# Routing of a fused attention, expert and feed-forward kernel: logits summed in PSUM, traced earlier

## The chip, the cores and the metric

One core of a Trainium2 chip runs the whole program. The metric is the device time of one execution in microseconds (us), lower is better; a profiled execution also has a trace of every instruction on TensorE (PE and its weight loads, PEld), VectorE (DVE), ScalarE (ACT), GpSimd (POOL) and the DMA-issuing queues (SP and ACT).

## The reference, cut to what matters

Three layers follow one another on 2304 tokens (4 batches of 576) of width 512. The routing of the second layer is what the change touches.

```python
# 1. attention with random features: q, k, v of shape (4, 8, 576, 64)
x = attn_out.transpose(0, 2, 1, 3).reshape(2304, 512)
# 2. experts: one of 8 per token, by the largest logit
logits = x @ w_gate                                # (2304, 8)
expert_idx = np.argmax(logits, axis=1)
probs = np.exp(logits - logits.max(-1, keepdims=True))
probs /= probs.sum(-1, keepdims=True) + 1e-09
gate_w = probs[np.arange(N), expert_idx]
for e in range(8):
    mask = expert_idx == e
    out[mask] = gate_w[mask, None] * (np.maximum(x[mask] @ w1[e], 0) @ w2[e])
# 3. feed-forward: h = y @ w_in; g = h * sigmoid(1.702 h); g @ w_out
```

## The kernel before, in words

The kernel works batch by batch and assumes that most tokens of a batch go to one expert: `route(b)` finds the expert that most of the 576 tokens chose, SyncE (the SP queue) reads its number into a register, and the weights of that expert alone are loaded and used for the whole batch. Tokens that chose another expert are counted in `total` and handled by a loop at the end, which runs only if there are any.

Attention is cut into 8 quads (a batch has two): `kgen(i)` makes the keys' side of a quad and `qgen(i)` the queries' side, in the order of the string `Q_ORDER`, where P is a projection with its row maximum (`ph_P`), X a transposition, N the product with its division, R the transposition into the expert layer's input (`xh`, `xl`). Each P step passes small results through the tile `small`, one whole PSUM bank with tag "t": its reduction writes there and two tensor operations read or write there (lines 359 and 368). Tag "n" is one other PSUM bank; `num` of the N steps, `kv_ps` of the keys, half of `lT_ps`, and in the routing `lg_ps` and `ct_ps` take it in turn, so each waits until the one before has been read. Tag "u" is a third one, shared by `tq`, `tx` and the other half of `lT_ps`.

Routing of batch b (`route_steps`) runs once both quads of the batch are done. It multiplies the inputs with the two halves of the gate weights (`wgs`, a rounded part and the rest, so 16 rows for 8 experts) into `lT`, turns `lT` with five transposes into `lg_ps` (tokens on partitions), copies that to SBUF, clears the 64 partitions of the last tile that hold no token, adds the two halves to `lg`, takes the row maximum `rm` and the one-hot `oh`, counts with a matmul by ones into `ct_ps`, and takes the index of the largest count (`es`). The gates (a softmax, `ex` and `gate`) and a per-token index (`lix`, five pairs of `max` and `max_index`) come along the way. Only after all this does the trace call `values_load` of `es` and `pump()`, which asks for the weights.

Two generators are interleaved by hand: attention `A` (with the routings) and the expert layer `Mg`. Inside attention `merge` takes the part that has the smallest ratio of steps taken to its weight: 17 for `qgen`, `ROUTE_N` for the routing, 5 for `kgen`. So `ROUTE_N = 10` spreads the routing's seven steps over the first six tenths of a quad; a larger number puts them closer to its start. Until the first routing is traced, only attention is traced; what has been traced by then is the `lead`, and from there on attention and experts alternate by cost. Routings of batches 0, 1 and 2 are merged into quads 2, 4 and 6; that of batch 3 follows all quads.

The order on each engine is not the traced one. The framework's scheduler plays the program through with its own durations, takes on each engine what is ready, and among that what was traced first; the order that it finds is then fixed, and each engine keeps to it, waiting in place where something is late. The SP queue carries the loads, the stores, the turning of the halves (`dma_start_transpose`, line 309), the register read and the loads of the expert weights, all in one such order. Loads of the first batch's weights are marked as high priority (`HP_STAGE`).

Of the kernel before, what the change touches and what calls it, by code (L numbers as in the profile page):

```python
# [8 lines left out]
F32 = mybir.dt.float32  # L9
# [13 lines left out]
def kernel(  # L23
# [13 lines left out]
    nc = tc.nc  # L37
    B, H, S, D = q.shape
    M = omega.shape[0]
    E, DM, F1 = w1.shape  # L40
    F2 = w_in.shape[1]
    NT = B * S
    P = 128
    T = 4
    TAIL = S - T * P
# [16 lines left out]
    XQ = nc.sync  # L62
    DVE_LO = 1
    KPRE = 6
    ROUTE_N = 10
    HP_ROUTE = 0
    HP_SPLIT = (0, 3)
    HP_STAGE = (0,)
# [438 lines left out]


    gate_t, reg_t = {}, {}

    def route(b):
        g = route_steps(b)
# [7 lines left out]
    def route_steps(b):  # L520
        yield 0
        xh, xl = xh_t[b], xl_t[b]
        lT = att.tile([2 * E, S], F32, tag="dg", name="lT", bufs=1)
        for hf, tg in ((0, "n"), (1, "u")):
            c = slice(hf * HS, (hf + 1) * HS)
            lT_ps = pp.tile([2 * E, HS], F32, tag=tg, name="lT_ps", bufs=1)
            for kk in range(KD):
                wk = wgs[:, kk].rearrange("p a e -> p (a e)")
                nc.tensor.matmul(out=lT_ps, lhsT=wk, rhs=xh[:, kk, c], start=(kk == 0), stop=False)
                nc.tensor.matmul(out=lT_ps, lhsT=wk, rhs=xl[:, kk, c], start=False, stop=(kk == KD - 1))  # L530
            nc.scalar.activation(out=lT[:, c], in_=lT_ps, func=ACTF.Copy)
        yield 2.0
        yield 0
        lg_ps = pp.tile([P, T + 1, 2, E], F32, tag="n", name="lg_ps", bufs=1)
        for t in range(T + 1):
            n = P if t < T else TAIL
            nc.tensor.transpose(
                lg_ps[:n, t].rearrange("p a e -> p (a e)"), lT[:, t * P:t * P + n], ident[:2 * E, :2 * E]
            )
        lg2 = att.tile([P, T + 1, 2, E], F32, tag="lg2", name="lg2", bufs=1)  # L540
        nc.vector.memset(lg2[:, T], 0.0)
        nc.vector.tensor_copy(lg2[:, 0:T], lg_ps[:, 0:T])
        nc.vector.tensor_copy(lg2[:TAIL, T], lg_ps[:TAIL, T])
        lg = att.tile([P, T + 1, E], F32, tag="lg", name="lg", bufs=1)
        nc.vector.tensor_tensor(out=lg, in0=lg2[:, :, 0], in1=lg2[:, :, 1], op=ALU.add)


        rm = att.tile([P, T + 1, 1], F32, tag="rm", name="rm", bufs=2)
        nc.vector.tensor_reduce(out=rm, in_=lg, axis=AX.X, op=ALU.max)
        oh = att.tile([P, T + 1, E], F32, tag="oh", name="oh", bufs=2)  # L550
        nc.vector.tensor_tensor(out=oh, in0=lg, in1=rm.to_broadcast([P, T + 1, E]), op=ALU.is_equal)
        nc.vector.memset(oh[TAIL:, T, :], 0.0)
        ex = att.tile([P, T + 1, E], F32, tag="ex", name="ex", bufs=2)
        nc.vector.tensor_tensor(
            out=ex, in0=lg, in1=rm.to_broadcast([P, T + 1, E]), op=ALU.subtract
        )
        nc.scalar.activation(out=ex, in_=ex, func=ACTF.Exp)
        yield 0.5
        yield 0
        ct_ps = pp.tile([P, T + 1, E], F32, tag="n", name="ct_ps", bufs=1)  # L560
        nc.tensor.matmul(
            out=ct_ps.rearrange("p t e -> p (t e)"), lhsT=ones, rhs=oh.rearrange("p t e -> p (t e)")
        )
        ct = att.tile([P, E], F32, tag="ct", name="ct", bufs=2)
        nc.vector.tensor_reduce(out=ct, in_=ct_ps.rearrange("p t e -> p e t"), axis=AX.X, op=ALU.add)
        cm = att.tile([P, 8], F32, tag="cm", name="cm", bufs=2)
        ci = att.tile([P, 8], U32, tag="ci", name="ci", bufs=2)
        nc.vector.max(cm, ct)
        nc.vector.max_index(ci, cm, ct)
        es = att.tile([P, 1], I32, tag="es", name="es", bufs=B)  # L570
        nc.vector.tensor_copy(es, ci[:, 0:1])
        gate = att.tile([P, T + 1, 1], F32, tag="gate", name="gate", bufs=2)
        nc.vector.tensor_reduce(out=gate, in_=ex, axis=AX.X, op=ALU.add)
        nc.vector.tensor_scalar(out=gate, in0=gate, scalar1=1e-9, scalar2=None, op0=ALU.add)
        nc.vector.reciprocal(out=gate, in_=gate)
        if b == B - 1:
            dg = att.tile([P, T * P + TAIL], F32, tag="dg", name="dg", bufs=1)
            for t in range(T + 1):
                n = P if t < T else TAIL
                nc.scalar.activation(  # L580
                    out=dg[:n, t * P:t * P + n], in_=ident[:n, :n], func=ACTF.Copy, scale=gate[:n, t, :]
                )
        cif = att.tile([P, 1], F32, tag="cif", name="cif", bufs=2)
        nc.vector.tensor_copy(cif, ci[:, 0:1])
        mx = att.tile([P, T + 1, 8], F32, tag="lmx", name="lmx", bufs=1)
        ix = att.tile([P, T + 1, 8], U32, tag="lix", name="lix", bufs=1)
        for t in range(T + 1):
            nc.vector.max(mx[:, t], lg[:, t])
            nc.vector.max_index(ix[:, t], mx[:, t], lg[:, t])
        ixf = att.tile([P, T + 1, 1], F32, tag="ixf", name="ixf", bufs=1)  # L590
        nc.vector.tensor_copy(ixf, ix[:, :, 0:1])
        eq = att.tile([P, T + 1, 1], F32, tag="eq", name="eq", bufs=1)
        nc.vector.tensor_scalar(out=eq, in0=ixf, scalar1=cif[:, 0:1], scalar2=None, op0=ALU.is_equal)
        nc.vector.memset(eq[TAIL:, T, :], 0.0)
        rr = att.tile([P, T + 1, 2], F32, tag="rr", name="rr", bufs=2)
        nc.vector.scalar_tensor_tensor(
            out=rr[:, :, 0:1], in0=eq, scalar=-float(2 * E), in1=ixf, op0=ALU.mult, op1=ALU.add
        )
        hit = att.tile([P, 1], F32, tag="hit", name="hit", bufs=1)
        nc.vector.tensor_reduce(out=hit, in_=eq.rearrange("p t o -> p (t o)"), axis=AX.X, op=ALU.add)  # L600
        nc.vector.tensor_tensor(out=total, in0=total, in1=hit, op=ALU.subtract)
        nc.vector.tensor_copy(rr[:, :, 1:2], gate)
        yield 0.5
        reg_t[b] = nc.values_load(
            es[0:1, 0:1], engines=[mybir.EngineType.SP], min_val=0, max_val=E - 1,
            skip_runtime_bounds_check_because="an index of the largest of E counts",
        )
        pump()
        nc.sync.dma_start(
            out=r_dram[b * S:b * S + T * P].rearrange("(p t) c -> p t c", t=T), in_=rr[:, 0:T]  # L610
        )
        nc.sync.dma_start(out=r_dram[b * S + T * P:(b + 1) * S], in_=rr[:TAIL, T])
        gb = moe.tile([P, S], F32, tag="gb", name="gb", bufs=2)
        if b < B - 1:
            row = att.tile([P, P, T + 1], F32, tag="dg", name="row", bufs=1)

            def leave():
                behind(nc.scalar.dma_start(out=gate_dram[b].rearrange("(p t) -> p t", p=P), in_=gate[:, :, 0]), 1)

# [24 lines left out]
        yield 1.1
# [355 lines left out]
    if True:  # L1000
# [544 lines left out]
```

## Time and profile before

| | us |
|---|---|
| three runs | 767.65, 767.72, 769.79 |
| median | 767.72 |
| the profiled execution | 767.65 |
| its span, first to last instruction | 765.6 |
| PE busy in the span | 739.7 |
| DVE busy | 531.3 |
| ACT busy | 338.6 |
| POOL busy | 131.9 |

The profiled execution has 2.05 us outside its span. Mean granted TensorE clock is 0.990. A busy PE is not a PE at its peak: matmuls are pipelined, and their ends are modelled. A duration of a single matmul is longer than the distance to the next one, so distances are taken from the chain, where each piece begins at the end of the piece before it.

### The profile page before, as it was taken

How to read it: one execution, taken by the hardware profiler on the slowest of the kernel's cores; microseconds unless marked ns; L12 is line 12 of the kernel's file. 1: busy time of each engine (PE TensorE's matmuls, PEld its weight loads, DVE VectorE, ACT ScalarE, POOL GpSimd, SP SyncE). 2: the span in 40 equal slices, each digit the busy share in tenths (PEclk: the TensorE clock that was granted, in tenths of full speed). 3: DMA queues.
4: the chain of work that ended last, by engine and by line, in shares of the span. 5: the costliest groups of instructions: out<-in, count | busy, mean ns of one | idle time of the engine just before them, and what ended most of it. 6: DMA issues, size and time to landing. Idle time of an engine off the chain costs nothing.

```text
span 765.6 us, 14359 instructions
## 1 busy us (share of the span) xinstructions
PE 739.7 (97%) x5559; PEld 716.1 (94%) x5559; DVE 531.3 (69%) x1188; ACT 338.6 (44%) x638; POOL 131.9 (17%) x78
## 2 busy tenths in 40 slices
PE   7998799999999999989999999999999999999997
PEld 6877699999999999979999999999999999999996
DVE  5867867586776685556879559981368777777774
ACT  5554464335522332233427464554576433444331
POOL 3563377609500441000000000000000000000000
PEclk9999799999999999999999999999999999999999
DMA  5447594456725554198145558972978544443311
GB/s 157 117 131 187 123 302 97 120 140 193 189 60 162 150 179 134 51 234 287 59 161 197 177 171 295 316 263 100 332 273 298 172 138 138 137 129 117 115 29 32
DMA packets 136715, 127.57 MB, mean 167 GB/s; under 512 B 58176, under 2 KB 120896, under 8 KB 135744
## 3 DMA queue, kind: packets, MB, share of 16 engines
q1 hardware_dynamic: 123936, 98.85, 43.5%
q10 hardware_dynamic: 12704, 27.73, 10.3%
q8 instruction: 45, 0.74, 0.4%
q14 instruction: 30, 0.25, 0.1%
HBM read 79.68 MB, written 40.40 MB: 157 GB/s over the span
## 4 chain that ended last, share of the span: by engine, by line
PE 83%; DVE 8%; DMA 4%; issue 1%; ACT 1%; SPq 1%; POOL 0%; ACTq 0%; POOLq 0%; DVEq 0%
PE m_ps L136 19%; PE qa L1249 13%; PE qa L1146 13%; PE qm L1249 7%; PE w_ps L136 4%; PE pb L1249 3%; PE qm L1146 3%; PE qu L1146 3%; PE num L444 3%; PE kv_ps L402 3%; DMA st<-in_moe_w_dram 2%; PE qn L1146 2%; PE qt L1146 2%; PE tq L430 1%; PE pr L344 1%
## 5 line engine op out<-in xcount | busy, mean ns | idle before, releaser
L1146 PE MATMUL qa<-y,wi 128*128 128x384 f32 x576 | 109.2, 337 | 0.4 <-DVE g L901 0.4
L1146 PEld LDWEIGHTS qa<-y,wi 128*128 128x128 f32 x576 | 101.4, 188 | 0.8 <-DVE g L901 0.8
L136 PE MATMUL m_ps<-xh,wh 128*128 128x288 f32 x256 | 79.0, 309 | 4.1 <-DVE h1l L735 2.3
L136 PE MATMUL m_ps<-xh,wl 128*128 128x288 f32 x256 | 76.8, 300 | 0.1
L136 PE MATMUL m_ps<-xl,wh 128*128 128x288 f32 x256 | 76.4, 298 | 0.0
L700 POOL TENSOR_TENSOR wl<-st,wh 128x1024 fp32r<-128x1024 f32 x23 | 55.1, 2401 | 83.0 <-ACT wh L698 82.9
L359 DVE TENSOR_REDUCE small<-pr 128x4 f32<-128x512 f32 (+1 forms) x80 | 51.1, 639 | 11.8 <-PE pr L351 7.8
L698 ACT ACTIVATE wh<-st 128x1024 fp32r<-128x1024 f32 (+1 forms) x33 | 34.0, 1035 | 48.5 <-DMA st<-in_moe_w_dram 31.6
L136 PEld LDWEIGHTS m_ps<-xh,wh 128*128 128x128 f32 x256 | 48.6, 190 | 5.8 <-DVE h1l L735 3.6
L136 PE MATMUL m_ps<-h1h,wh 128*128 128x288 f32 x160 | 48.8, 305 | 0.9 <-DVE h1l L735 0.9
L136 PEld LDWEIGHTS m_ps<-xh,wl 128*128 128x128 f32 x256 | 48.6, 190 | 0.5 <-DVE wl L700 0.4
L735 DVE SCALAR_TENSOR_TENSOR h1l<-m_ps,h1h 128x288 fp32r<-128x288 f32 x64 | 28.9, 453 | 28.9 <-ACT h1h L732 28.8
L136 PEld LDWEIGHTS m_ps<-xl,wh 128*128 128x128 f32 x256 | 48.6, 190 | 0.0
L136 PE MATMUL m_ps<-h1l,wh 128*128 128x288 f32 x160 | 47.7, 298 | 0.0
L136 PE MATMUL m_ps<-h1h,wl 128*128 128x288 f32 x160 | 47.4, 298 | 0.0
L732 ACT ACTIVATE h1h<-m_ps 128x288 fp32r<-128x288 f32 x64 | 25.9, 407 | 48.5 <-PE m_ps L136 46.7
L1249 PE MATMUL qa<-p,p 128*128 128x256 f32 x360 | 46.2, 282 | 1.1 <-DVE p L855 0.8
L1249 PE MATMUL qa<-p,gs 128*128 128x256 f32 x360 | 45.9, 282 | 0.0
L1249 PEld LDWEIGHTS qa<-p,p 128*128 128x128 f32 x360 | 44.2, 189 | 1.6 <-DVE p L855 1.0
L1249 PEld LDWEIGHTS qa<-p,gs 128*128 128x128 f32 x360 | 44.2, 189 | 0.0
L444 PEld LDWEIGHTS num<-kv,qpT 128*128 128x128 f32 (+1 forms) x320 | 36.7, 184 | 5.4 <-ACT qpT L432 3.1
L444 PE MATMUL num<-kv,qpT 128*128 128x65 f32 (+1 forms) x320 | 39.3, 266 | 2.5 <-ACT qpT L432 1.4
(213 smaller groups left out, 1819.5 us busy)
## 6 DMA issues: line engine op xcount, KB each, us to landing
g_dram<-g ACTq DMA_DIRECT2D x48, 384.0 KB, 4.1
st<-in_moe_w_dram SPq DMA_DIRECT2D x31, 512.0 KB, 5.2
pg<-g_dram SPq DMA_DIRECT2D x10, 1024.0 KB, 5.7
raw<-in_moe_w_in_dram SPq DMA_DIRECT2D x16, 512.0 KB, 4.0
gt<-g_dram SPq DMA_DIRECT2D x8, 1024.0 KB, 5.4
p<-wo_dram SPq DMA_DIRECT2D x6, 1024.0 KB, 7.3
yt<-y_dram SPq DMA_DIRECT2D x12, 384.0 KB, 6.0
vm<-in_v_dram SPq DMA_DIRECT2D x32, 128.0 KB, 3.2
```

What stands on the lines that cost most here:

```text
L136: ins = nc.tensor.matmul(out=ps, lhsT=a, rhs=b, start=start and n == 0, stop=stop and n == 2)
L344: nc.tensor.matmul(out=ps[:, :, h2], lhsT=xT[:, (2 * pr + h2) * 2 + t0 // 2], rhs=wbd)
L359: nc.vector.tensor_reduce(out=pm, in_=ps[:, :w], axis=AX.X, op=ALU.max, negate=on_act)
L402: nc.tensor.matmul(out=kv_ps[:, h, :], lhsT=kp[j // 2][:, j % 2, h2, :], rhs=vm[:, h, t, :], start=(t == 0), stop=False,)
L430: nc.tensor.transpose(tq[:, c, h2], qp[i][:, c, h2, :], ident)
L444: nc.tensor.matmul(out=ps[:n, c, h2, :], lhsT=lhsT, rhs=kv[:, h, :])
L698: nc.scalar.activation(out=hi[:, :, s], in_=st[:, :, s], func=ACTF.Copy)
L700: eng.tensor_tensor(out=lo[:, :, s], in0=st[:, :, s], in1=f32(hi)[:, :, s], op=ALU.subtract)
L732: nc.scalar.activation(out=hh[:, f], in_=ps, func=ACTF.Relu)
L735: nc.vector.scalar_tensor_tensor(out=hl[:, f], in0=ps, scalar=0.0, in1=f32(hh[:, f]), op0=ALU.max, op1=ALU.subtract)
L1146: ins = nc.tensor.matmul(out=ps, lhsT=w[:, a, ks], rhs=y[:, b, kk], start=start and kk + m == 0, stop=kk == 1 and m == 2, skip_group_check ...
L1249: ins = nc.tensor.matmul(out=ps, lhsT=x[:, f], rhs=w[i][:, f], start=start and f + m == 0, stop=f == NP - 1 and m == 2, skip_group_check=True,
```

## The change

Logits: five transposes of `lT` become five matmuls of `lT` with `fold`, a 16x8 matrix of two identities, which turns and adds the two halves at once; the result stays in PSUM, in columns 256 to 295 of `small`, and the maximum, the one-hot and the gates' subtraction read it there. `lT` is widened to 640 columns and the last 64 are cleared, so nothing has to be cleared behind it. Counts: a matmul over the first four tiles and one over the 64 real tokens of the last, into columns 384 to 423 of `small`. The register read and `pump()` move up, directly behind `es`; the gates come after them. The per-token index comes from the one-hot by a multiplication with 8, 7, ... 1 and a maximum (`left`) instead of five pairs of `max` and `max_index`. `ROUTE_N` goes from 10 to 40. Two small operations at the start of the program make `fold` and `left`.

```diff
-    ROUTE_N = 10
+    ROUTE_N = 40
...
+    lgx = att.tile([P, 2, E], F32, name="lgx")
+    fold, left = lgx[:2 * E, 0], lgx[:, 1]
+
+    def setup_route():
+        nc.vector.tensor_tensor(out=fold, in0=ident[:2 * E, 0:E], in1=ident[:2 * E, E:2 * E], op=ALU.add)
+        nc.vector.tensor_scalar(out=left, in0=iota8, scalar1=-1.0, scalar2=float(E), op0=ALU.mult, op1=ALU.add)
...
-        lT = att.tile([2 * E, S], F32, tag="dg", name="lT", bufs=1)
+        lT = att.tile([2 * E, (T + 1) * P], F32, tag="dg", name="lT", bufs=1)
+        nc.vector.memset(lT[:, S:], 0.0)
...
-        lg_ps = pp.tile([P, T + 1, 2, E], F32, tag="n", name="lg_ps", bufs=1)
+        lg_ps, ct_ps = (
+            small[:, x:x + (T + 1) * E].rearrange("p (t e) -> p t e", e=E) for x in (2 * P, 3 * P)
+        )
         for t in range(T + 1):
-            n = P if t < T else TAIL
-            nc.tensor.transpose(
-                lg_ps[:n, t].rearrange("p a e -> p (a e)"), lT[:, t * P:t * P + n], ident[:2 * E, :2 * E]
-            )
-        lg2 = att.tile([P, T + 1, 2, E], F32, tag="lg2", name="lg2", bufs=1)
-        nc.vector.memset(lg2[:, T], 0.0)
-        nc.vector.tensor_copy(lg2[:, 0:T], lg_ps[:, 0:T])
-        nc.vector.tensor_copy(lg2[:TAIL, T], lg_ps[:TAIL, T])
-        lg = att.tile([P, T + 1, E], F32, tag="lg", name="lg", bufs=1)
-        nc.vector.tensor_tensor(out=lg, in0=lg2[:, :, 0], in1=lg2[:, :, 1], op=ALU.add)
+            nc.tensor.matmul(out=lg_ps[:, t], lhsT=lT[:, t * P:(t + 1) * P], rhs=fold)
...
-        nc.vector.memset(oh[TAIL:, T, :], 0.0)
...
-        ct_ps = pp.tile([P, T + 1, E], F32, tag="n", name="ct_ps", bufs=1)
         nc.tensor.matmul(
-            out=ct_ps.rearrange("p t e -> p (t e)"), lhsT=ones, rhs=oh.rearrange("p t e -> p (t e)")
+            out=ct_ps[:, 0:T].rearrange("p t e -> p (t e)"), lhsT=ones, rhs=oh[:, 0:T].rearrange("p t e -> p (t e)")
         )
+        nc.tensor.matmul(out=ct_ps[:, T], lhsT=ones[:TAIL, :], rhs=oh[:TAIL, T])
...
         nc.vector.tensor_copy(es, ci[:, 0:1])
+        reg_t[b] = nc.values_load(es[0:1, 0:1], engines=[mybir.EngineType.SP], ...)
+        pump()
+        ex = att.tile([P, T + 1, E], F32, tag="ex", name="ex", bufs=2)
+        nc.vector.tensor_tensor(out=ex, in0=lg_ps, in1=rm.to_broadcast([P, T + 1, E]), op=ALU.subtract)
+        nc.scalar.activation(out=ex, in_=ex, func=ACTF.Exp)
...
-        for t in range(T + 1):
-            nc.vector.max(mx[:, t], lg[:, t])
-            nc.vector.max_index(ix[:, t], mx[:, t], lg[:, t])
         ixf = att.tile([P, T + 1, 1], F32, tag="ixf", name="ixf", bufs=1)
-        nc.vector.tensor_copy(ixf, ix[:, :, 0:1])
+        nc.vector.tensor_tensor(out=oh, in0=oh, in1=left.unsqueeze(1).to_broadcast([P, T + 1, E]), op=ALU.mult)
+        nc.vector.tensor_reduce(out=ixf, in_=oh, axis=AX.X, op=ALU.max)
+        nc.vector.tensor_scalar(out=ixf, in0=ixf, scalar1=-1.0, scalar2=float(E), op0=ALU.mult, op1=ALU.add)
...
-        reg_t[b] = nc.values_load(es[0:1, 0:1], engines=[mybir.EngineType.SP], ...)
-        pump()
...
         setup_wg()
+        setup_route()
```

## Rows read from the trace of the kernel before

**Rows 1.** The page, busy time and share of the span by engine.

```profile
PE 739.7 (97%) x5559; PEld 716.1 (94%) x5559; DVE 531.3 (69%) x1188; ACT 338.6 (44%) x638; POOL 131.9 (17%) x78
```

**Rows 2.** Busy time of each engine by stretch, then granted clock, DMA share, GB/s.

```profile
73.50:79.00 5.50, 4.38 (x48) 3.61 (x47) 4.94 (x18) 3.98 (x10) 4.90 (x3) 1.00 0.05 10
79.00:86.00 7.00, 4.90 (x41) 4.04 (x39) 6.92 (x43) 2.57 (x8) 3.50 (x3) 0.76 0.38 87
86.00:95.00 9.00, 5.94 (x43) 5.05 (x43) 5.92 (x27) 3.24 (x11) 0.00 (x0) 0.79 0.71 170
95.00:98.00 3.00, 2.98 (x14) 2.83 (x15) 2.06 (x6) 2.74 (x8) 0.33 (x1) 0.50 1.04 349
...
110.00:270.00 160.00, 160.00 (x1422) 154.02 (x1421) 110.14 (x358) 64.38 (x123) 69.61 (x33) 1.00 0.53 144
...
330.00:350.00 20.00, 17.56 (x124) 16.65 (x125) 13.63 (x23) 6.35 (x10) 0.00 (x0) 1.00 0.89 235
```

**Rows 3.** The chain that ended last, around the first routing: start, us, what.

```profile
73.41 0.70 ACT lT L531 x2
...
77.91 0.06 PE pr L350
...
78.25 0.38 PE lg_ps L537 x5
...
88.35 0.06 DVE es L571
...
89.22 4.37 DMA st<-in_moe_w_dram
...
95.02 2.77 PE m_ps L136 x10
...
98.42 0.45 PE num L444 x4
```

**Rows 4.** PE in order of time; idle before and its releaser in brackets.

```profile
75.55 1.11 PE L444 MATMUL num<-kv,qpT 128*128 128x65 f32 x8 [0.75 <-ACT qpT L432]
...
80.01 1.08 PE L444 MATMUL num<-kv,qpT 128*128 128x65 f32 x8 [0.83 <-DVE small L368]
...
84.98 0.39 PE L561 MATMUL ct_ps<-oh,ones 128*128 128x40 f32 x2 [0.76 <-DVE xn L455]
...
94.30 0.40 PE L136 MATMUL m_ps<-xh,wh 128*128 128x288 f32 x1 [1.73 <-ACT wh L698]
```

**Rows 5.** DVE in order of time.

```profile
74.42 0.70 DVE L359 TENSOR_REDUCE small<-pr 128x4 f32<-128x512 f32 x1
...
75.36 0.16 DVE L368 TENSOR_TENSOR mx<-small,sq 128x4 f32<-128x4 f32 x1
...
77.11 0.42 DVE L455 TENSOR_TENSOR xn<-num,rd 128x256 f32<-128x256 f32 x1
...
79.90 1.35 DVE L545 TENSOR_TENSOR lg<-lg 128x40 f32<-128x40 f32 x1
...
84.42 0.42 DVE L455 TENSOR_TENSOR xn<-num,rd 128x256 f32<-128x256 f32 x1
```

**Rows 6.** The SP queue in order of time.

```profile
82.01 5.73 SPq L309 DMA_TRANSPOSE xT<-hl  x2
```

**Rows 7.** What the SP queue waited for, 72 to 90 us: total, times, longest.

```profile
SPq L309 <- PE pr L351: 11.3, 2, 9.4
```

**Rows 8.** The tile lg, all four routings: ns min/median/max, first and last start.

```profile
L588 DVE MAX8 lmx<-lg x20: 145/153/160, 81.4 to 317.0; 128x8 f32<-128x8 f32 x20
L589 DVE MATCH_VALUE_LOAD lix<-lmx,lg x20: 71/73/88, 82.7 to 318.2; 128x8 f32 x20
L589 DVE FIND_INDEX8 lix<-lmx,lg x20: 154/160/171, 82.8 to 318.3; 128x8 uint32<-128x8 f32 x20
```

**Rows 9.** Groups by line and shape: count, busy us, mean ns, idle before, releaser.

```profile
L700 DVE TENSOR_TENSOR wl<-st,wh 128x1024 fp32r<-128x1024 f32 x8 | 9.8, 1224 | 7.1 <-ACT wh L698 7.1
```

More of the change, by code (lines that the diff above doesn't have):

```diff
@@ L533, in route_steps @@
         yield 0
-        lg_ps = pp.tile([P, T + 1, 2, E], F32, tag="n", name="lg_ps", bufs=1)
+        lg_ps, ct_ps = (
+            small[:, x:x + (T + 1) * E].rearrange("p (t e) -> p t e", e=E) for x in (2 * P, 3 * P)
+        )
         for t in range(T + 1):
-            n = P if t < T else TAIL
-            nc.tensor.transpose(
-                lg_ps[:n, t].rearrange("p a e -> p (a e)"), lT[:, t * P:t * P + n], ident[:2 * E, :2 * E]
-            )
-        lg2 = att.tile([P, T + 1, 2, E], F32, tag="lg2", name="lg2", bufs=1)
-        nc.vector.memset(lg2[:, T], 0.0)
-        nc.vector.tensor_copy(lg2[:, 0:T], lg_ps[:, 0:T])
-        nc.vector.tensor_copy(lg2[:TAIL, T], lg_ps[:TAIL, T])
-        lg = att.tile([P, T + 1, E], F32, tag="lg", name="lg", bufs=1)
-        nc.vector.tensor_tensor(out=lg, in0=lg2[:, :, 0], in1=lg2[:, :, 1], op=ALU.add)
+            nc.tensor.matmul(out=lg_ps[:, t], lhsT=lT[:, t * P:(t + 1) * P], rhs=fold)
         rm = att.tile([P, T + 1, 1], F32, tag="rm", name="rm", bufs=2)
-        nc.vector.tensor_reduce(out=rm, in_=lg, axis=AX.X, op=ALU.max)
+        nc.vector.tensor_reduce(out=rm, in_=lg_ps, axis=AX.X, op=ALU.max)
         oh = att.tile([P, T + 1, E], F32, tag="oh", name="oh", bufs=2)
-        nc.vector.tensor_tensor(out=oh, in0=lg, in1=rm.to_broadcast([P, T + 1, E]), op=ALU.is_equal)
-        nc.vector.memset(oh[TAIL:, T, :], 0.0)
[L553 to L557, printed above, removed]
+        nc.vector.tensor_tensor(out=oh, in0=lg_ps, in1=rm.to_broadcast([P, T + 1, E]), op=ALU.is_equal)
         yield 0.5
         yield 0
-        ct_ps = pp.tile([P, T + 1, E], F32, tag="n", name="ct_ps", bufs=1)
         nc.tensor.matmul(
-            out=ct_ps.rearrange("p t e -> p (t e)"), lhsT=ones, rhs=oh.rearrange("p t e -> p (t e)")
+            out=ct_ps[:, 0:T].rearrange("p t e -> p (t e)"), lhsT=ones, rhs=oh[:, 0:T].rearrange("p t e -> p (t e)")
         )
+        nc.tensor.matmul(out=ct_ps[:, T], lhsT=ones[:TAIL, :], rhs=oh[:TAIL, T])
         ct = att.tile([P, E], F32, tag="ct", name="ct", bufs=2)
@@ L571, in route_steps @@
         nc.vector.tensor_copy(es, ci[:, 0:1])
+        reg_t[b] = nc.values_load(
+            es[0:1, 0:1], engines=[mybir.EngineType.SP], min_val=0, max_val=E - 1,
+            skip_runtime_bounds_check_because="an index of the largest of E counts",
+        )
+        pump()
+        ex = att.tile([P, T + 1, E], F32, tag="ex", name="ex", bufs=2)
+        nc.vector.tensor_tensor(
+            out=ex, in0=lg_ps, in1=rm.to_broadcast([P, T + 1, E]), op=ALU.subtract
+        )
+        nc.scalar.activation(out=ex, in_=ex, func=ACTF.Exp)
         gate = att.tile([P, T + 1, 1], F32, tag="gate", name="gate", bufs=2)
@@ L584, in route_steps @@
         nc.vector.tensor_copy(cif, ci[:, 0:1])
-        mx = att.tile([P, T + 1, 8], F32, tag="lmx", name="lmx", bufs=1)
-        ix = att.tile([P, T + 1, 8], U32, tag="lix", name="lix", bufs=1)
-        for t in range(T + 1):
-            nc.vector.max(mx[:, t], lg[:, t])
-            nc.vector.max_index(ix[:, t], mx[:, t], lg[:, t])
         ixf = att.tile([P, T + 1, 1], F32, tag="ixf", name="ixf", bufs=1)
-        nc.vector.tensor_copy(ixf, ix[:, :, 0:1])
+        nc.vector.tensor_tensor(out=oh, in0=oh, in1=left.unsqueeze(1).to_broadcast([P, T + 1, E]), op=ALU.mult)
+        nc.vector.tensor_reduce(out=ixf, in_=oh, axis=AX.X, op=ALU.max)
+        nc.vector.tensor_scalar(out=ixf, in0=ixf, scalar1=-1.0, scalar2=float(E), op0=ALU.mult, op1=ALU.add)
         eq = att.tile([P, T + 1, 1], F32, tag="eq", name="eq", bufs=1)
@@ L603, in route_steps @@
         yield 0.5
[L604 to L607, printed above, removed]
-        pump()
         nc.sync.dma_start(
```

## The prediction

> **What bounds the kernel now.** I began with the page's busy table: TensorE works in 97% of the span, no other engine in more than 69% [rows 1]. So a change can save only where TensorE stands or runs at its lower clock, and costs wherever it adds TensorE work to a stretch that is already full. The table by stretches then shows where that is [rows 2]. From 110 to 270 us TensorE is busy 160.00 of 160.00 us at clock 1.00; nothing is to be won there. Around the first routing it is not: from 73.5 to 79 it is busy 4.38 of 5.50, from 79 to 86 4.90 of 7.00 at clock 0.76, from 86 to 95 5.94 of 9.00 at clock 0.79, and the first expert matmuls run at 0.50, which is 1.2 of 2.4 GHz. VectorE is busy 6.92 of 7.00 from 79 to 86, so attention alone can't fill TensorE there: it is bound by VectorE. The second loose place is 330 to 350, with 20.00 - 17.56 = 2.44 us idle.
>
> The chain through the first place says what ends last [rows 3]. `lT` is evicted by 74.11. The five transposes follow only at 78.25, the index `es` is made at 88.35, the weights are asked for at 89.22 and land 4.37 us later, and the expert stream sets in at 95.02. TensorE's own timeline shows it standing for these weights last (1.73 us before 94.30) [rows 4]. From the end of `lT` to `es` are 14.2 us for operations that take some 2 us themselves.
>
> Why they take so long is read off TensorE's and VectorE's timelines together. `num` of the first N step takes the "n" bank at 75.55 [rows 4] and is read out by VectorE from 77.11 to 77.53 [rows 5]; only then can `lg_ps` have the bank, 4 us after `lT` is there. The next `num` waits 0.83 us in turn for the copies out of `lg_ps`, and the count matmul waits 0.76 us for the division that ends at 84.84 [rows 4, 5]. In between the add of the two halves takes 1.35 us [rows 5], and the operations of P steps that were traced earlier take their turns on VectorE.
>
> **The change part by part.**
>
> *Off the "n" bank, and traced earlier.* With a weight of 40 the logits are traced behind the second P step of the quad and the counts behind the first X step, ahead of the N steps; in `small` no `num` has to be read out first. I take it that logits must still wait for the P steps traced before them, since these use the same bank: the third of them ends at 75.36 + 0.16 = 75.52 [rows 5]. From there: ten TensorE instructions (an f32 matmul appears as two, as the counts do [rows 4]) at 0.11 us each, from `num`'s 0.45 for 4 [rows 3], are 1.1; maximum, one-hot, count reduction and `es` at some 0.17 us each, the price of such small operations (`max` 0.153, index 0.160, load 0.073 [rows 8]), with one index search come to 1.1; four count instructions 0.4. Waiting behind one VectorE operation of up to 0.70 us [rows 5] at each of four hops is 0 to 2.8, and I take 1.2. `es` is then made at about 79.3 instead of 88.35, 9 us earlier; the bounds are 7 and 10. The register read and eight weight loads come with it, and the expert stream sets in at about 86.0.
>
> *What the shift is worth.* In 86 to 95 TensorE's busy time at the granted clock is 5.94 x 0.79 = 4.7 us, so 4.3 are free; by counting, its 43 instructions at 0.06 to 0.11 us apart [rows 3] are 2.6 to 4.7, so 4.3 to 6.4 are free. Expert matmuls, which need nothing but weights, fill that: I take 4.9. If the shift is 7 us, 3.3. The ten slow matmuls at 95.02 (2.77 us) I expect again, at the new place, since the stretch ahead of them stays sparse; if the clock stays up, 1.4 more is gained.
>
> *VectorE's work.* Per routing go five `max` and index pairs, 5 x (0.153 + 0.073 + 0.160) = 1.93 us [rows 8], two copies, two memsets, one cast and the add, some 0.8 more by the prices of small operations, and for the first routing the add's long 1.35 [rows 5]. A memset, a multiplication, a reduction and a scalar operation come in, 0.6. So 2.1 us a routing, 3.3 in the first. Where TensorE is full this is worth nothing, since VectorE is off the path. In 73.5 to 86, where VectorE is the bound, attention comes forward by up to 3.3 us, which at 4.90 x 0.76 us of TensorE work in 7.00 [rows 2] is 1.7 at most; as the experts soon fill that stretch anyway, I take 1.0.
>
> *TensorE's added work.* Five transposes at 0.38 [rows 3] become ten instructions: 0.76 if each takes as long as a transpose, 1.1 at `num`'s price; the counts go from two instructions to four, 0.15 to 0.22. That is 0.5 to 0.9 a routing. In the first it falls into free time; the other three lie where TensorE is full [rows 2]: 1.6 to 2.8, and I take 2.0.
>
> *Reading logits in PSUM, gates behind the index, two setup operations.* Gates are first needed at the end of the experts' first stage, half a batch away, and the setup is two small operations at the program's start; nothing, or 0.3 us if the start stands for them. The SP queue now has the register read and the weight loads ahead of what was traced later, its two turned-halves transfers above all (82.01 to 87.74 [rows 6]); these serve the next quads and may start some 3 us later, which the expert matmuls cover. Without that cover they would delay the next P step by as much, up to 3 us.
>
> *Last routing.* It stays behind all quads in the trace, so only its own shortening counts. Of the 2.44 us idle at 330 to 350 I take 1.0 back; bounds 0 and 2.4.
>
> *Waits on `small`.* Logits and counts on TensorE stand behind VectorE's use of that bank, and P steps behind theirs. The waits on "n" that go were 0.83 and 0.76; I take 0.5 us more in the full stretches, bounds 0 and 6 x 1.1 (a whole P step, 74.42 to 75.52 [rows 5]).
>
> Sum: -4.9 - 1.0 + 2.0 - 1.0 + 0.5 = -4.4 us. The profiled execution took 767.65, which gives 763.2; it lies 0.07 below the median shown, so the same number serves for both.
>
> **The rivals.** *The SP queue keeps the old place.* The two transfers at line 309 stand at its head, waiting 9.4 us for P matmuls to free a buffer [rows 7], and the second ends at 87.74 [rows 6]. If the scheduler leaves the register read behind them, the early index is worth under 1 us of shift, 0.5 us of time, and the sum is -0.5 - 1.0 + 2.0 - 1.0 + 0.5: 767.7, no change. For it: they were traced first. Against it: they wait until 82.0, and the index should be there at 79.3 with loads of high priority. Between the two transfers the shift would be about 4 us, and 765.
>
> *The shared bank becomes the wait: slower.* Each P step now locks TensorE's logits and counts and is locked by them. In the six places of the last three routings TensorE keeps its order and would stand for a P step (1.1 us) and, where one is ahead of it, a long VectorE operation (1.22 [rows 9]), with all expert matmuls queued behind. From 0.8 us a place (4.9 in all, where 0.5 was taken) the gain is gone; at 1.5 us it is 763.2 + 8.5 = 771.7. For it: at 80 and 85 us TensorE did stand 0.83 and 0.76 for exactly such a hand-over. Against: the scheduler puts an instruction where it expects it to be ready, and in 110 to 270 TensorE never stands, although "n" is shared in the same way.
> The Trainium skill speaks for this rival: PSUM — Partial Sum Buffer, "PSUM bank collisions raise a hardware error", asks that two engines be kept apart by bank and quadrant, not by address, so different columns of `small` don't make logits and P steps independent. Were the rule not applied here, logits could start at 74.15 rather than 75.52, and the sum would be some 0.7 us lower. No row here shows two engines in that bank at once, which agrees with the rule and doesn't prove it.
>
> *The new order costs elsewhere.* All that is traced after the lead moves (the lead is about ten trace steps shorter), so prefetches and hand-overs fall differently; either sign, some 2 us.
>
> **How the numbers follow.** Forecast 0.57 (its own range 760.0 to 765.5), SP queue 0.18 (765 to 768.5), bank 0.15 (768.5 to 772), new order 0.10, half of it at each side of no change. 0.3%, 2.3 us, is about what a measurement of this kernel can tell from no change: the three runs differ by 2.1. Faster by more than that, below 765.4: most of the forecast, a little of the SP rival and of the last: 0.59. Slower, above 770.0: most of the bank and a part of the last: 0.16. Between: 0.25. The range leaves out the strongest form of the bank rival and the very best: bounds at their best (-6.4 for the shift, -1.7, +1.6, -1.0) give 760.1, and with the clock up 758.7; I take 759.5 to 769.0.
>
> **What would show it.** Right: no wait of `num` or `ct_ps` for the "n" bank; `es` near 79 and the first weights asked for near 80, ahead of line 309 on SP; the first expert matmul near 85 instead of 94.30; TensorE's idle time from 73.5 to 98 some 4 us shorter; logits as ten instructions in about 1 us. Wrong: weights still asked for behind 87 (the queue); TensorE idle in 110 to 270 ahead of `small` (the bank); or that stretch kept and the saved time gone again before 350.

## The result, and the profile after

The rebuilt routing is slower: 778.87 us, the median of 4 runs (777.09 to 781.43), against 767.68 of before, ratio 1.0141, 95% interval [1.0112, 1.0169]. Forecast was 763.2. The profiled execution took 777.57 with a span of 775.6, 10.0 more than before.

The page of the kernel after, and the stretches of [rows 2] (us, busy PE, PEld, DVE, ACT, POOL, then granted clock, DMA share, GB/s):

```profile
PE 746.7 (96%) x5587; PEld 723.4 (93%) x5587; DVE 520.3 (67%) x1122; ACT 337.2 (43%) x638; POOL 131.7 (17%) x78
```

```profile
73.50:79.00 5.50, 4.72 (x27) 3.09 (x25) 3.55 (x10) 2.53 (x5) 3.60 (x4) 0.69 0.16 36
79.00:86.00 7.00, 6.39 (x43) 6.06 (x43) 3.64 (x19) 1.78 (x6) 5.86 (x3) 0.61 0.01 2
86.00:95.00 9.00, 6.98 (x45) 6.07 (x45) 7.48 (x34) 3.91 (x9) 0.49 (x1) 0.55 0.74 234
95.00:98.00 3.00, 3.00 (x29) 3.00 (x28) 2.04 (x4) 3.00 (x6) 3.00 (x2) 1.00 1.06 389
110.00:270.00 160.00, 154.38 (x1364) 147.41 (x1364) 98.79 (x322) 59.94 (x116) 62.65 (x30) 0.99 0.56 138
330.00:350.00 20.00, 20.00 (x151) 19.75 (x150) 15.81 (x47) 9.69 (x21) 0.00 (x0) 1.00 0.72 210
```

The clock had fallen before the first logits, in a stretch of 2 us from 74 on:

```profile
74.00:76.00 2.00, 2.00 (x11) 1.02 (x9) 1.83 (x5) 0.80 (x2) 1.92 (x2) 0.50 0.26 58
```

Read against [rows 2]: from 79 to 86 VectorE, which was full there (6.92 of 7.00), is busy 3.64; the clock is 0.55 to 0.69 for 21 us where it was 0.76 to 1.00 (the next 3 us run at 1.00 where they ran at 0.50); and 110 to 270, full before, has 5.6 us idle. TensorE has 28 instructions more, seven for each routing.

TensorE, then VectorE, around the first routing (start, us, engine, line, operation; in brackets the idle time ahead and what ended it):

```profile
75.37 0.33 PE L350 MATMUL pr<-wh,xT 128*128 128x128 f16 x1
...
77.92 1.11 PE L444 MATMUL num<-kv,qpT 128*128 128x65 f32 x8 [0.75 <-ACT qpT L432]
78.95 1.28 PE L545 MATMUL small<-lgx,lT 16*128 16x8 f32 x10
...
82.39 0.58 PE L552 MATMUL small<-oh,ones 128*128 128x32 f32 x2
82.90 0.59 PE L555 MATMUL small<-oh,ones 64*128 64x8 f32 x2
...
86.79 0.27 PE L350 MATMUL pr<-wh,xT 128*128 128x128 f16 x1 [1.40 <-DVE qp L380]
...
88.62 1.10 PE L444 MATMUL num<-kv,qpT 128*64 128x65 f32 x8 [0.82 <-DVE xn L455]
...
90.13 0.61 PE L136 MATMUL m_ps<-xh,wh 128*128 128x288 f32 x1 [0.41 <-ACT wh L692]
```

```profile
80.27 0.20 DVE L547 TENSOR_REDUCE rm<-small 128x5 f32<-128x40 f32 x1 [0.37 <-PE small L545]
80.50 0.20 DVE L549 TENSOR_TENSOR oh<-small,rm 128x40 f32<-128x40 f32 x1
83.53 0.20 DVE L557 TENSOR_REDUCE ct<-small 128x8 f32<-128x40 f32 x1 [2.83 <-PE small L555]
83.65 0.19 DVE L570 TENSOR_TENSOR ex<-small,rm 128x40 f32<-128x40 f32 x1
83.75 1.32 DVE L588 TENSOR_TENSOR oh<-oh,lgx 128x40 f32<-128x40 f32 x1
85.00 0.16 DVE L560 MAX8 cm<-ct 128x8 f32<-128x8 f32 x1
85.08 0.41 DVE L359 TENSOR_REDUCE small<-pr 128x2 f32<-128x256 f32 x1
...
85.87 0.14 DVE L563 CAST es<-ci 128x1 int32<-128x1 uint32 x1
```

`es` comes at 85.87, some 2.4 us earlier than before (88.26 on VectorE's timeline), not 9. VectorE stands 2.83 us for the counts. The next P reduction, which writes the same bank, comes only at 85.08, although its matmuls began at 75.37; TensorE then stands 1.40 us for the `qp` of that P step. VectorE's waits on routing results in the whole run (total us, times, longest):

```profile
DVE rm L547 <- PE small L545: 7.0, 3, 5.1
DVE ct L557 <- PE small L555: 4.3, 3, 2.8
```

One more difference lies ahead of the routing altogether. The turnings of the halves on SP's queue, first before, then after, in two quads of the attention that come before any routing:

```profile
57.34 1.89 SPq L309 DMA_TRANSPOSE xT<-hl  x1
...
61.00 2.40 SPq L309 DMA_TRANSPOSE xT<-hl  x1
```

```profile
56.88 2.73 SPq L309 DMA_TRANSPOSE xT<-hl  x1
...
60.77 3.31 SPq L309 DMA_TRANSPOSE xT<-hl  x1
```

Nothing in the order of the instructions explains that; e7 to e12 below look for the cause.

All is lost before the feed-forward layer: its first matmul starts at 400.4 before and 410.7 after, and the rest takes 365.2 and 364.9. What the time up to that matmul consists of, from stretches of 2 us each: idle TensorE, time lost at the lower clock (length x (1 - granted clock)), and the remainder, which is TensorE's work at full clock. There is one profile of each kernel, and runs of one kernel differ by some 3 to 10 us, so a difference of 1 or 2 us in a column says little.

| kernel | idle | lost at lower clock | work |
|---|---|---|---|
| before | 18.7 | 6.8 | 374.9 |
| after | 22.1 | 12.0 | 376.7 |
| e1, weight 40 alone | 17.8 | 6.8 | 370.8 |
| e5, e1 with the shared bank | 22.2 | 6.8 | 373.4 |
| e9, e14, one-hot index, `hl` on its boundary | 20.2, 19.2 | 6.8, 5.1 | 373.3, 373.3 |
| e4, after with banks n and u | 19.0 | 10.3 | 377.4 |
| e11, after, `hl` on its boundary | 22.0 | 8.5 | 376.8 |
| e12, the same with banks n and u | 17.7 | 6.8 | 378.7 |
| e13, TensorE's part alone | 18.0 | 10.2 | 378.1 |

### The profile page after: what moved, and what is told of

Same layout as the page of the kernel before. It is cut to its first block, busy times and chain, and to the rows that moved or that the text cites. A ratio compares the mean times of both kernels' runs of the same rounds, so it can differ in the third digit from the quotient of the medians.

```text
span 775.6 us, 14360 instructions
## 1 busy us (share of the span) xinstructions
PE 746.7 (96%) x5587; PEld 723.4 (93%) x5587; DVE 520.3 (67%) x1122; ACT 337.2 (43%) x638; POOL 131.7 (17%) x78
## 4 chain that ended last, share of the span: by engine, by line
PE 80%; DMA 9%; DVE 4%; ACT 2%; SPq 2%; issue 2%; POOL 0%; ACTq 0%; DVEq 0%
PE m_ps L136 16%; PE qa L1244 13%; PE qa L1141 13%; PE qm L1244 7%; DMA st<-in_moe_w_dram 5%; PE w_ps L136 4%; PE pb L1244 3%; PE qm L1141 3%; PE qu L1141 3%; PE num L444 3%; DMA m<-in_q_dram 2%; PE tq L430 2%; PE kv_ps L402 2%; PE qn L1141 2%; PE pr L344 2%
```

## The experiments

Ratios are to the kernel before, run beside each kernel on the same chip, with 95% intervals; e1 to e4 ran on one chip, e5 to e8 on a second, e9 to e15 on a third. There were three theories at first: Q (the order of SP's queue costs the time), B (the bank that the routing shares with the P steps), T (the work added on TensorE and VectorE).

Four pairs below turn out to be the same program twice. Where an edit only moves `values_load` and `pump()` in the source (e3 against after, e6 against e1, e8 against e4, e14 against e9), the scheduler puts the register read and the loads back where they were. In the built programs the two kernels of a pair have the same instructions in the same order on every engine, and their traces show SyncE's instructions and TensorE's matmuls in the same order (after and e3: 623 and 5587). Their ratios differ by up to 0.3% (1.0141 and 1.0113), so smaller differences between two ratios are not taken for effects here.

**e1: the weight alone.** Before, with one line changed.

```diff
-    ROUTE_N = 10
+    ROUTE_N = 40
```

> The kernel before with ROUTE_N = 40 alone; routing as it was. Theory Q (the register read and the eight weight loads go onto the SP queue ahead of the two line-309 transfers, so the next quads' data come late and attention starves from 110 us): those transfers are issued near 93 and 100 us instead of 82 and 86, TensorE idles 4 to 6 us between 110 and 270, and the time is 775 to 780. Theory B (logits and counts in the bank of the P steps are the cost): no change of bank here, so 765 to 769. Theory T (added TensorE and changed VectorE work is the cost): 765 to 769.

763.47 (7 runs), ratio 0.9975 [0.9944, 1.0005]. The register read comes at 81.7, the first expert matmul at 85.98 instead of 94.30, and the turnings at line 309 start at 90.24 and 97.98 instead of both from 82.01 on [rows 6]. So the old routing, traced earlier, brings the expert matmuls 8 us forward by itself, and turnings 8 us late cost no time on the whole. The gain is 2 us, not the 4.9 that the prediction gave to such a shift, and by this run alone it is not clear of noise (e6, the same program, is). In the trace the free time moved forward and was not filled. Ahead of the counts TensorE now stands 5.01 us for the one-hot, and from 73 to 100 it loses 10.8 us idle or at the lower clock, against 11.4 before.

```profile
77.60 0.62 PE L561 MATMUL ct_ps<-oh,ones 128*128 128x40 f32 x2 [5.01 <-DVE oh L552]
```

**e2: all but the weight.** After, with one line changed back.

```diff
-    ROUTE_N = 40
+    ROUTE_N = 10
```

> The changed kernel with ROUTE_N = 10; all of the rebuilt routing stays. Theory Q: the scheduler has both line-309 transfers ahead of the register read again, so 764 to 769, faster than before by what the shorter routing is worth. Theory B: logits and counts still lie in the bank of the P steps, so 774 to 780. Theory T: the added TensorE work is still there, 769 to 772.

777.27, ratio 1.0139 [1.0112, 1.0166], as slow as after, although the turnings start at 82.01 and 87.82 as before, ahead of the register read. Theory Q falls with e1 and e2 together.

**e3: the register read late.** After, with `values_load` and `pump()` where they were.

```diff
@@ behind es
-        reg_t[b] = nc.values_load(es[0:1, 0:1], ...)
-        pump()
@@ behind the last yield, ahead of the stores to r_dram
+        reg_t[b] = nc.values_load(es[0:1, 0:1], ...)
+        pump()
```

> The changed kernel with the register read and the weight loads traced behind the gates, where they were before; ROUTE_N stays 40. Theory Q: the read stands ahead of the line-309 transfers on SP as in the changed kernel, so 775 to 780, no gain. A theory that the early read within the routing is the cost expects 765 to 769. Theory B: 775 to 780 as well.

774.53, ratio 1.0113 [1.0080, 1.0147]. This is the program of after once more, so it can't tell what an early read costs, only how far two measurements of one program lie apart. It also means that one part of the change, the read moved up in the source, had no effect.

**e4: own banks** (as the labels call them: logits go to n, which `num` uses too, and counts to u, which `tq` uses too).

```diff
-        lg_ps, ct_ps = (small[...] for x in (2 * P, 3 * P))
+        lg_ps = pp.tile([P, T + 1, E], F32, tag="n", name="lg_ps", bufs=1)
...
+        ct_ps = pp.tile([P, T + 1, E], F32, tag="u", name="ct_ps", bufs=1)
```

> The changed kernel with logits in bank n and counts in bank u instead of the tile small. Theory Q: same order on SP, so 775 to 782. Theory B: the waits on the shared bank go, 764 to 769.

770.22 (10 runs), ratio 1.0059 [1.0042, 1.0076]: 0.8% comes back (0.5% by e3). VectorE's two waits shrink from 7.0 and 4.3 to 0.7 us each, while its waits for the matmuls of P steps grow, the largest group from 6.2 to 10.9. After, then e4:

```profile
DVE small L359 <- PE pr L351: 6.2, 4, 3.3
...
DVE small L359 <- PE pr L351: 10.9, 10, 3.3
...
DVE rm L545 <- PE lg_ps L543: 0.7, 2, 0.5
DVE ct L556 <- PE ct_ps L554: 0.7, 1, 0.7
```

Theory B holds for about half of the loss or more, and not for the rest.

**e5: the bank alone.** e1, with transposed logits and counts in `small`, nothing else of the change.

```diff
-        lg_ps = pp.tile([P, T + 1, 2, E], F32, tag="n", name="lg_ps", bufs=1)
+        lg_ps = small[:, 2 * P:2 * P + 2 * (T + 1) * E].rearrange("p (t a e) -> p t a e", a=2, e=E)
...
-        ct_ps = pp.tile([P, T + 1, E], F32, tag="n", name="ct_ps", bufs=1)
+        ct_ps = small[:, 3 * P:3 * P + (T + 1) * E].rearrange("p (t e) -> p t e", e=E)
```

> The kernel before with a weight of 40, and of the rest of the change only the place: transposed logits and counts go to columns 256 to 335 and 384 to 423 of `small`; the copies to SBUF, the clearing, the five index pairs and the late register read stay. Theory B (the shared bank makes VectorE stand behind TensorE's logits and counts, with the P reductions queued behind): some 6 to 9 us over the weight of 40 alone, ratio to the kernel before 1.004 to 1.010, and VectorE again waits several us on `small` at the copy of the logits and the count reduction. Rival H (not the place, but how long the bank is held: three readings of the logits in PSUM, the last for the gates): at most 3 us over the weight of 40 alone, ratio 0.996 to 1.001.

769.59 (11 runs), ratio 1.0056 [1.0031, 1.0080], 0.8% over e1: the place costs it, with the old copies to SBUF. VectorE waits on it again:

```profile
DVE lg L542 <- PE small L537: 5.5, 3, 4.5
DVE ct L565 <- PE small L561: 1.2, 2, 0.8
```

In e1 the same copy waited 1.8 us in four times. Rival H falls. A new place also gives the scheduler another order: TensorE's matmuls in e1 and e5 part ways from the first routing on. How much of the 0.8% is waiting in the bank itself, and how much the order that the bank leads to, was not separated.

**e6: the early read alone.** e1, with the edit of e3 turned round: `values_load` and `pump()` directly behind `es`.

> The kernel before with a weight of 40, and of the rest only the register read with the asking for weights directly behind `es`. Theory R (an early read blocks the queue of SP, which then stands for the index with the turned halves behind it): 2 to 4 us over the weight of 40 alone, ratio 1.000 to 1.003. Rival: the scheduler puts it where it was, no difference, ratio 0.996 to 0.999, with the register read at 81 to 82 us as with the weight alone.

763.45 (12 runs), ratio 0.9967 [0.9949, 0.9985]. This is e1's program again, as the rival said: the scheduler put the read where it was. So the run does not test theory R; but as the order of after is the same with the late read of e3, nothing of the loss is due to an early one. What the run does give is a second measure of e1, and by it the gain of the weight is clear of noise.

**e7: the one-hot index alone.** e1, with this alone (and `left`, made at the program's start).

```diff
+    left = att.tile([P, E], F32, name="left")
...
-        for t in range(T + 1):
-            nc.vector.max(mx[:, t], lg[:, t])
-            nc.vector.max_index(ix[:, t], mx[:, t], lg[:, t])
-        nc.vector.tensor_copy(ixf, ix[:, :, 0:1])
+        nc.vector.tensor_tensor(out=oh, in0=oh, in1=left.unsqueeze(1).to_broadcast([P, T + 1, E]), op=ALU.mult)
+        nc.vector.tensor_reduce(out=ixf, in_=oh, axis=AX.X, op=ALU.max)
+        nc.vector.tensor_scalar(out=ixf, in0=ixf, scalar1=-1.0, scalar2=float(E), op0=ALU.mult, op1=ALU.add)
```

> The kernel before with a weight of 40, and of the rest only the index by multiplication and maximum in place of the five pairs of maximum and index. By my forecast (VectorE's work saved around the first routing): 1 us under the weight of 40 alone, ratio 0.995 to 0.998. Rival (two-input operations on SBUF take 1.2 us and more beside a GpSimd operation and stand in the way there): equal to it or up to 2 us over, ratio 0.998 to 1.001.

769.77 (12 runs), ratio 1.0044 [1.0028, 1.0061], 0.7% over e1, outside both expectations. Three operations of 0.15 to 0.19 us on VectorE (one of them once 0.60) don't explain 5 us. The trace shows the loss ahead of the first routing: TensorE's order up to `lT_ps` is that of e1, but the turnings take longer, and the matmul behind them on the way to `lT_ps` waits. SP, then TensorE, of e7:

```profile
56.73 2.73 SPq L309 DMA_TRANSPOSE xT<-hl  x1
...
60.62 3.19 SPq L309 DMA_TRANSPOSE xT<-hl  x1
```

```profile
70.78 0.37 PE L466 MATMUL small<-ident,xn 64*128 64x64 f32 x1 [1.66 <-DVE xl L473]
```

In e1 that matmul did not wait. Over before, after and e1 to e8 the turnings that start at 55 to 63 us fall in two groups: 1.8 to 1.9 and 2.3 to 2.4 us in before, e1, e5 and e6, 2.7 and 3.2 to 3.4 in after, e2 to e4, e7 and e8. What the second group has in common is a new tile, `lgx` (64 bytes a partition) or `left` (32), allocated ahead of `hl`. In the compiled program `hl` begins at byte 76800 of a partition (300 x 256) in the first group, and 64 or 32 bytes off a multiple of 256 in the second.

**e8: own banks and a late read.** e4 and e3 together.

> The kernel after with its logits in a tile of tag n and its counts in one of tag u, and the register read at its old place: both suspects undone, all else of the change kept. If bank and early read add up (8.7 and 2 to 4 us of the 11 us lost): 763 to 767, ratio 0.994 to 0.999, at or a little over the weight of 40 alone. Rival A (TensorE's added instructions and the new order cost the rest): 769 to 771, ratio 1.002 to 1.006, the same as with own banks alone.

770.77 (7 runs), ratio 1.0056 [1.0036, 1.0076], no better than e4. It is e4's program again, so the number is that of rival A without bearing it out; against e3 it gives the bank 0.6%.

**e9 to e12: the layout.** e9 is e7 with `left` made 256 bytes wide, e11 is after and e12 is e4 with `lgx` made so; the instructions and their order on every engine stay, which the built programs bear out. e10 is e1 with an unused tile of 32 bytes.

```diff
-    lgx = att.tile([P, 2, E], F32, name="lgx")
+    lgx = att.tile([P, 8, E], F32, name="lgx")
@@ e10
-    gate_t, reg_t = {}, {}
+    gate_t, reg_t, pad = {}, {}, att.tile([P, E], F32, name="pad")
```

> The kernel of e7 (weight of 40, index by the one-hot), with the tile that holds 8, 7, ... 1 made 256 bytes wide instead of 32, so that `hl` begins at a multiple of 256 bytes again; order and instructions are those of e7. Theory L (layout: every turning of halves at line 309 is slower where `hl` lies off a multiple of 256 bytes, 2.73 us against 1.87 at the first quads, and that is the whole cost of e7): the first transfers take 1.9 to 2.4 us again and the ratio is 0.994 to 0.999, that of the weight of 40 alone or a little better. Rival O (the one-hot operations themselves are dear): unchanged, 1.003 to 1.006.

> The kernel before with a weight of 40 and an unused tile of 32 bytes ahead of `hl`, nothing else; order and instructions are those of e1. Theory L: the transfers at line 309 take 2.7 us at the first quads, where e1 has 1.86, and the ratio is 1.002 to 1.007. Rival: an unused tile changes nothing, 0.995 to 0.999.

> The kernel after, with its setup tile made 256 bytes wide instead of 64, so that `hl` begins at a multiple of 256 bytes; order and instructions on every engine are those of the kernel after. If layout and shared bank add up (0.7% and 0.8%): ratio 1.004 to 1.009. If the bank was all of it: 1.012 to 1.017. If the layout was all of it: 0.995 to 1.000.

> The kernel of e4 (after, with logits and counts in banks n and u), with the setup tile made 256 bytes wide: both causes undone, all else of the change kept. If layout and bank are the whole loss: ratio 0.993 to 0.999. If something else of the change costs as well (TensorE's added instructions, 2 us by my forecast): 0.999 to 1.003.

All turnings of a run (ns, shortest/median/longest) in e1, e10, e7, e9, after and e11:

```profile
L309 SPq DMA_TRANSPOSE xT<-hl x11: 1777/2136/7006, 34.6 to 202.2; - x11
```

```profile
L309 SPq DMA_TRANSPOSE xT<-hl x11: 2493/2869/6893, 34.5 to 201.8; - x11
```

```profile
L309 SPq DMA_TRANSPOSE xT<-hl x11: 2485/2837/6900, 35.3 to 210.2; - x11
```

```profile
L309 SPq DMA_TRANSPOSE xT<-hl x11: 1770/2079/7742, 34.9 to 205.8; - x11
```

```profile
L309 SPq DMA_TRANSPOSE xT<-hl x11: 2732/3277/6817, 34.8 to 212.8; - x11
```

```profile
L309 SPq DMA_TRANSPOSE xT<-hl x11: 1839/2166/6920, 34.4 to 209.8; - x11
```

The address decides over the turnings, both ways: 32 bytes in front of `hl` lift the shortest from 1.78 to 2.49 us, 224 more bring it back. In e10, with e1's order, the matmul of e7's trace waits as well (1.55 us at 69.50). In time: e9 0.9978 [0.9957, 0.9999] against 1.0044 of e7, so its whole loss; e11 1.0104 [1.0062, 1.0146] against 1.0141; e12 1.0027 [1.0003, 1.0050] against 1.0059 of e4. e10 gives 0.9996 [0.9975, 1.0017] against 0.9975 of e1: the transfers are as slow as foretold, the time moves less than foretold, and the two intervals overlap, as do those of after and e11 and of e4 and e12. By after and e3 against e11 the layout of the kernel after is worth 0.4% or 0.1%, by e4 and e8 against e12 0.3%; I take 0.1% to 0.4%. That it costs the kernel time is clear in e7 against e9, and only likely for the others. All tiles behind the new one moved with `hl`, and no run moved `hl` alone, so that the whole time comes through the turnings is not shown. Between e11 and e12 the bank is worth 0.8% again, with the orders of after and e4.

The Trainium skill, DMA: Bandwidth & Descriptors, "How a descriptor splits into AXI transactions", says that a transaction must begin at a multiple of 256 bytes, so that the first one of a descriptor that doesn't begins at the boundary below and pays for bytes that it does not use. `hl`'s rows for one turning are 128 f16 values, 256 bytes. The trace agrees in direction, with 0.7 to 0.9 us a turning; no run shows the transactions themselves. The destination is not the cause: `xT` begins on a multiple of 256 in after, where turnings are slow, and off it in before.

**e13: TensorE's part alone.** e1, with ten logits instructions through `fold` and four for the counts, in bank n, `hl` on its boundary; one copy of the logits replaces VectorE's two copies, add and clearing, since they are folded already.

```diff
-            nc.tensor.transpose(lg_ps[:n, t]..., lT[:, t * P:t * P + n], ident[:2 * E, :2 * E])
+            nc.tensor.matmul(out=lg_ps[:, t], lhsT=lT[:, t * P:(t + 1) * P], rhs=fold)
...
+        nc.tensor.matmul(out=ct_ps[:, T], lhsT=ones[:TAIL, :], rhs=oh[:TAIL, T])
```

> The kernel before with a weight of 40, and of the rest only TensorE's part: ten matmul instructions with `fold` in place of five transposes and counts in four instructions in place of two, both in bank n as before, `hl` kept on a multiple of 256 bytes, the logits copied to SBUF by one copy. Theory T (in the trace of e12 the ten logits take 1.21 us against 0.38 for five transposes, the counts about 0.6 against 0.14, so 1.3 us a routing, 3.9 to 5.2 in all): ratio 1.001 to 1.005. Rival (they fill gaps, and VectorE is relieved of copies and the add): ratio 0.995 to 0.999, that of the weight of 40 alone.

773.51 (12 runs, 767.43 to 777.98), ratio 1.0076 [1.0045, 1.0107]: more than theory T said. What T counted is in the traces. The second routing's logits in e9 (five transposes) and in e12 (ten instructions), with the next matmul behind them, and e12's counts:

```profile
154.34 0.45 PE L542 MATMUL lg_ps<-ident,lT 16*128 16x16 f32 x5
154.72 0.40 PE L136 MATMUL m_ps<-xl,wh 128*128 128x288 f32 x1
```

```profile
155.39 1.28 PE L543 MATMUL lg_ps<-lgx,lT 16*128 16x8 f32 x10
156.60 0.40 PE L136 MATMUL m_ps<-xh,wh 128*128 128x288 f32 x1
...
159.85 0.36 PE L551 MATMUL ct_ps<-oh,ones 128*128 128x32 f32 x2
160.14 0.39 PE L554 MATMUL ct_ps<-oh,ones 64*128 64x8 f32 x2
160.46 0.23 PE L351 MATMUL pr<-wl,xT 128*128 128x128 f16 x1
```

0.38 us became 1.21, and the counts 0.61, where e9's two instructions take 0.14: 1.30 us more a routing, 5.2 in four. The column "work" of the table says the same: 376.7 to 378.7 with `fold`, 370.8 to 374.9 without. What e13 lost beyond that, its profiled run shows in one place:

```profile
180.90 0.66 PE L464 MATMUL tx<-ident,xn 128*128 128x128 f32 x2 [4.10 <-DVE xl L473]
```

```profile
175.00:180.00 5.00, 1.80 (x15) 1.56 (x14) 0.00 (x0) 1.51 (x3) 2.67 (x2) 1.00 0.91 232
180.00:185.00 5.00, 4.10 (x16) 3.67 (x17) 2.19 (x7) 3.13 (x6) 3.83 (x2) 0.55 0.88 249
185.00:190.00 5.00, 5.00 (x26) 5.00 (x25) 4.06 (x11) 2.26 (x5) 3.88 (x3) 0.50 0.93 310
190.00:195.00 5.00, 5.00 (x26) 4.94 (x26) 0.71 (x4) 2.76 (x4) 5.00 (x3) 0.50 0.31 72
195.00:200.00 5.00, 5.00 (x38) 4.78 (x37) 3.29 (x11) 1.01 (x2) 5.00 (x4) 0.74 0.62 163
```

TensorE stood 4.1 us and then ran some 15 us at 0.50 to 0.55, 0.50 being the lower of its two levels. ScalarE had waited 3.65 us there for a load of expert weights, with `xh` queued behind it. Why that load is late in this order was not tried, nor whether it is so in every run. Without `fold` and the second count matmul, there is e14. It differs from e12 in more than that: e12's counts lie in bank u, where a `tq` waits 1.8 us for them, and e14 keeps the copies of the logits on VectorE.

**e14: the parts that cost nothing.** e9 with the early read.

> The kernel of e9 (weight of 40, one-hot index, `hl` on its boundary) with the register read and the asking for weights directly behind `es`: the parts of the change that no run showed to cost anything, with the transposes and the separate bank kept. If these parts add up: ratio 0.993 to 0.998. If they gain nothing beyond the weight of 40: 0.996 to 0.999, the same within the measurement.

764.85 (12 runs), ratio 0.9988 [0.9977, 1.0000], 0.4% under e12. It is e9's program again, and by e9 it is 0.5%. So TensorE's part costs some 0.4% (e12, with the limits just named) to 1.0% (e13, which includes the late load). Beyond the weight, the one-hot index gains nothing.

**e15: half of the bank.** e5, with the counts back in bank n.

> The kernel of e5 (weight of 40, transposed logits and counts in `small`), with the counts back in a tile of tag n. If it is the logits that make VectorE stand in `small`: ratio 1.003 to 1.008, as e5. If it is the counts: 0.996 to 0.999, that of the weight of 40 alone. If each does half: 1.000 to 1.003.

766.13 (12 runs), ratio 1.0008 [0.9994, 1.0023], between e1 and e5: logits and counts each seem to do about half.

The best version is the kernel before with `ROUTE_N = 40`, measured as e1 and as e6: 0.3% under before and 1.7% under after (1.0141 / 0.9967).

## Why the prediction was wrong

The forecast was 4.4 us faster, and it came 11.2 us slower. The loss of 1.4% (1.1% by e3) adds up nearly: -0.3 for the weight (e1, e6), +0.8 for the bank (e5 over e1, after over e4, e11 over e12; 0.6 by e3 over e8), +0.1 to +0.4 for the layout (after and e3 over e11, e4 over e12), +0.4 for TensorE's work (e12 over e14). That is 1.0 to 1.3; each term is good to some 0.3.

- **The step that failed: "Waits on `small` ... I take 0.5 us".** The bank costs 0.5 to 0.9%, 4 to 7 us, around the upper bound of 6.6 that the text gave this term. The prediction had this as a rival (771.7) but let TensorE stand for it. What the traces show is that VectorE stands: it keeps its order, so a P reduction stands with the count reduction, in the first routing until 85.08, and TensorE waits 1.40 us for what follows from it. Of idle TensorE there are 3.1 to 4.4 us more with the shared bank in all three pairs, and 0 to 1.7 us more at the lower clock. The sign that the text gave, TensorE idle ahead of `small` from 110 to 270, is not what the trace shows: of its 5.6 us there 5.5 wait for `h1l` (hidden values of the expert layer) and `qpT`.
- **What stays open in it.** Not every wait of VectorE costs time. The longest for logits (5.08 us, until 240.84) falls where TensorE is busy 15.00 of 15.00 us (230 to 245). The low clock of 73.5 to 95 is not the bank's alone, since it is 0.50 already at 74 to 76, ahead of the logits, behind 2.02 us in which TensorE waited for `xl` (until 71.57); with `hl` on its boundary and the bank still shared, 8.5 us are lost to the clock instead of 12.0.
- **"TensorE's added work ... I take 2.0".** A routing adds 1.30 us of TensorE's time where 0.5 to 0.9 was reckoned: ten logits take 1.21 against an upper bound of 1.1, and the counts 0.47 more instead of 0.15 to 0.22. In time that is some 3 us (e12 over e14), or 7.7 where a late load comes on top (e13 over e1).
- **"The setup is two small operations at the program's start; nothing".** It was their tile that cost: it moved `hl` off a 256-byte boundary, 0.1% to 0.4%. No part of the sum looked at addresses.
- **The shift, -4.9.** By `ROUTE_N` alone the expert weights do come 8 us earlier, as foretold (e1), but this is worth 2 us: TensorE now stands for the one-hot ahead of them. The early read had no part in it. In the kernel after, `es` came at 85.87 instead of 79.3: logits stood behind `tq` and `num` until 78.95, in part at the lower clock, counts behind eight P matmuls and a `tq`.
- **VectorE's relief, -1.0.** VectorE has 11 us less work ([rows 1] against 520.3), and no run shows a gain from it. The one-hot index, the part of it that was run alone, leaves e9 as fast as e1, no faster.
- **Last routing, -1.0.** The 2.44 us idle from 330 to 350 [rows 2] are gone, but from 350 to 370 TensorE is now busy 17.26 of 20.00 (before 19.20): 2.74 us idle in the two stretches against 3.24.
- **Right:** no wait of `num` or the counts behind a routing result in the "n" bank (`num` still waits 0.82 us at 88.62 for the `num` before it to be read out); the register read ahead of line 309 on SP; turnings late, though by 11.6 us (82.01 to 93.65), not 3, and without cost where they are 8 us late (e1); the rival of SP's queue was rightly held unlikely.

## What to carry to other kernels

A PSUM bank that two steps share ties their instruction streams together, at 0.5 to 0.9% here: before a result moves into a bank that another step uses, list which instructions on the reading engine are queued behind it. When a change adds a tile, look where the tiles behind it now begin; a pad that restores the old boundary separates the cost of a change from that of its layout, with the order of all instructions unchanged. Before an edit is credited with a time, compare the order of instructions with and without it: four kernels here were another one over again. And try the cheapest part alone first: here one number (`ROUTE_N`) held all of the gain.

## What the runs showed of the hardware

- A turning DMA of 18 blocks of 128 x 128 f16 halves from SBUF to SBUF takes 1.77 to 1.86 us at its shortest in a run when the source begins on a multiple of 256 bytes, 2.49 to 2.73 when it lies 32 or 64 bytes off.
- A small VectorE operation with two SBUF inputs (L588, 128 x 40) took 1.32 us at 83.75 and 0.19 in the other routings; GpSimd was at work (2.11 us from 81.44, 1.39 from 83.62). The add of the two halves in before had 1.35 [rows 5]. The Trainium skill, SBUF — State Buffer, "SBUF: two separate sides", has a VectorE operation with two SBUF inputs and a GpSimd operation that reads SBUF hold a shared port pair in turn, each for a whole instruction; the rows agree, but no run here took GpSimd's work away.
